# Turning the keys of a causal retention and gated-unit kernel by DMA instead of TensorE

## The chip, the cores and the metric

The kernel runs on one core of one Trainium2 chip. The metric is the device time of one execution in microseconds; the profile's span is a little shorter, since it begins with the first and ends with the last instruction on the engines. Engines are named as in the profile: PE is TensorE (PEld its weight loads), DVE is VectorE, ACT is ScalarE, POOL is GpSimd, SP is SyncE, which only issues DMAs. A small q behind an engine's name (SPq) means its queue of instructions that issue DMAs.

## The reference

The first part is retention: attention without softmax, in which the weight of a pair of positions decays with their distance. The second part is a gated linear unit whose gate is a causal convolution over five positions.

```python
# q, k, v: (8 batches, 8 heads, 576 positions, 64), float32
scores = q @ k.transpose(0, 1, 3, 2) / sqrt(64)
gamma  = 1 - 2 ** (-5 - arange(8))                 # one per head
Dmat   = where(i >= j, gamma ** (i - j), 0)        # i, j: positions
x      = ((scores * Dmat) @ v)                     # then heads side by side: (8, 576, 512)

gate_pre = sum(conv_w[kk] * x_padded[:, kk:kk + 576, :] for kk in range(5))
gate     = 1 / (1 + exp(-gate_pre))
val      = x @ w_val                               # w_val: 512 x 512
out      = (gate * val) @ w_out                    # w_out: 512 x 512, float32
```

## The kernel before

The positions are worked through in chunks of 128: four full ones in each batch, and the last 64 positions of two batches together as one "tail". That makes 36 chunks, numbered t = 0 to 35. Inside a chunk the scores are computed and masked; what earlier chunks contribute comes through a carried state (keys times values, summed). The decay is folded into the values (on GpSimd) and into the result.

For the scores TensorE needs queries and keys with the head dimension across the partitions, but they are loaded with the position there. So both are turned. Four transposes of 128x128 (two heads each) go through TensorE against an identity matrix into PSUM, and VectorE copies the result to SBUF (queries: ScalarE):

```python
        def turned(src, pool=None):                                   # L241 is the transpose below
            ps = pool.tile([P, NP, P], BF16, name="g") if pool else ps_t.tile([P, NP, P], BF16, name="tps")
            flat = src.rearrange("p h d -> p (h d)")
            for pr in range(NP):                                      # NP = 4
                nc.tensor.transpose(ps[:, pr, :], flat[:, pr * P:(pr + 1) * P], ident)
            return ps

        def turn_k(t, copy=nc.vector.tensor_copy):
            ps = turned(kbf[t])
            kt = tp_sb.tile([P, NP, P], BF16, name="kt")
            copy(kt, ps)                                              # L249
            ktd[t] = kt
```

Loads. Values (and the queries of tails) come through SyncE's queue in float32; the queries of the four full chunks of a batch come in one DMA of 1 MB. Keys come through GpSimd's queue, whose DMAs convert to bfloat16 on the way:

```python
        def load_one(name, src, kind, b, c, bufs):
            t = half.tile([P, H, D], F32, name=f"f{name}c", bufs=bufs)
            if kind == "full":
                nc.sync.dma_start(out=t, in_=src[b, :, c * P:(c + 1) * P, :].rearrange("h p d -> p h d"))
            # ... tails: two halves

        def load_keys(t):
            kb = bfp.tile([P, H, D], BF16, name="kb", bufs=LA + 3)    # LA = 8
            if kind == "full":
                nc.gpsimd.dma_start(out=kb, in_=k[b, :, c * P:(c + 1) * P, :].rearrange("h p d -> p h d"))
            # ... tails: two halves
            kbf[t] = kb
```

The first chunks are written out by hand, with much preparation between them. The steady part is this loop; each engine takes its own instructions out of it in this order. A unit n of the gated part covers two chunks; its convolution and value product run in an even iteration, its projection in the odd one after it.

```python
        for t in range(4, NT + 2):                                    # NT = 36
            n = t // 2 - 1
            # ...
            for b in qload.get(t, []):
                load_queries(b)                                       # SyncE, 1 MB
            if ok(t + LA - 2):
                load(t + LA - 2)                                      # SyncE: values of chunk t + 6
            if ok(t + 4):
                load_keys(t + 4)                                      # GpSimd
            if ok(t + 2):
                cast_v(t + 2)                                         # GpSimd: decay into the values
            for job in qjobs.get(t + 1, []):
                cast_q(job)                                           # GpSimd: queries to bfloat16
            if ok(t):
                take_state(t)
            if ok(t + 1):
                scores(t + 1)                                         # TensorE, needs ktd[t + 1]
                masks(t + 1, 0)
            if ok(t):
                values(t)
                if not odd:
                    take_x(t)
            # ... second mask
            if unit and not odd and n > 1:
                conv(n)                                               # TensorE, tiles of 64x64
                gate(n, 0)
                gate(n, 1)
            if ok(t + 2) and t > 4:
                turn_k(t + 2)                                         # TensorE and VectorE
            # ...
            part = project if odd else value
            if unit and t > 4:
                part(n, 0)
            # ...
            if jobs:
                turn_q(jobs[0])
            if unit and t > 4:
                part(n, 1)
            # ...
            if ok(t + 1):
                carried(t + 1)
                update(t + 1)
```

`project` ends with a copy on ScalarE and the store of 128 finished positions on SyncE's queue:

```python
            ob = op_sb.tile([P, DM], F32, name="ob")                  # 5 buffers
            nc.scalar.copy(ob, o)                                     # L414
            if kind == "full":
                c0 = (c + i) * P
                nc.sync.dma_start(out=out[b, c0:c0 + P, :], in_=ob)   # L417
```

Of the kernel before, what the change touches and what calls it, by code (L numbers as in the profile page):

```python
# [14 lines left out]
BF16 = mybir.dt.bfloat16  # L15
# [6 lines left out]
def kernel(  # L22
# [10 lines left out]
    nc = tc.nc  # L33
# [3 lines left out]
    P = 128  # L37
    NP = H // 2
# [13 lines left out]
    tp_sb = ctx.enter_context(tc.tile_pool(name="tsb", bufs=3))  # L52
# [16 lines left out]
    NT = len(chunks)  # L69

    with tc.manual_schedule():
# [13 lines left out]
        def load(t):  # L85
            kind, b, c = chunks[t]
            if kind == "tail":
                load_one("q", q, kind, b, c, 2)
            load_one("v", v, kind, b, c, LA + 1)

        def load_keys(t):

            kind, b, c = chunks[t]
            kb = bfp.tile([P, H, D], BF16, name="kb", bufs=LA + 3)
            if kind == "full":
                nc.gpsimd.dma_start(out=kb, in_=k[b, :, c * P:(c + 1) * P, :].rearrange("h p d -> p h d"))  # L96
            else:
                for i in range(2):
                    nc.gpsimd.dma_start(out=kb[i * TAIL:(i + 1) * TAIL],
                                        in_=k[b + i, :, c * P:S, :].rearrange("h p d -> p h d"))  # L100
            kbf[t] = kb

        kbf, vbf = {}, {}

        def load_queries(b):
            t = half.tile([P, H, RQ, D], F32, name="fqb", bufs=2)
            nc.sync.dma_start(out=t.rearrange("p h r d -> p h (r d)"),
                              in_=q[b, :, 0:RQ * P, :].rearrange("h (p r) d -> p h (r d)", r=RQ))
            loaded["qb", b] = t
# [109 lines left out]
        def cast_v(t, eng=nc.gpsimd):  # L219
            vb = bfp.tile([P, H, D], BF16, name="vb")  # L220
            eng.tensor_tensor(vb, loaded["v", *chunks[t]],  # L221
                                    gin[:, chunks[t][2], :].unsqueeze(2).to_broadcast([P, H, D]), op=ALU.mult)
            vbf[t] = vb
# [4 lines left out]
        def cast_q(job, copy=nc.gpsimd.tensor_copy):  # L228
            qb = bfp.tile([P, H, D], BF16, name="qb", bufs=5)
            if job[0] == "own":  # L230
                src = loaded["q", *chunks[job[1]]]
            else:
                src = loaded["qb", job[1]][:, :, job[2], :]
            copy(qb, src)  # L234
            qbf[job] = qb
# [6 lines left out]
            return ps  # L242

        ktd = {}

        def turn_k(t, copy=nc.vector.tensor_copy):
            ps = turned(kbf[t])
# [3 lines that stand above are left out]
# [22 lines left out]
        def scores(t, spare=False):  # L273
            kt = ktd[t]
            s = [ps_g.tile([P, NP, P], F32, name="g") if spare else ps_s.tile([P, NP, P], F32, name=f"s{i}")
                 for i in range(2)]
            for pr in range(NP):
                for i in range(2):
                    r = slice(i * 64, i * 64 + 64)
                    nc.tensor.matmul(s[i][:, pr, :], lhsT=kt[r, pr, :], rhs=queries(t, r, pr),  # L280
                                     start=(pr == 0), stop=(pr == NP - 1), skip_group_check=True)
            sps[t] = s
# [3 lines left out]
        def masks(t, i):  # L286
            m = mask_q if chunks[t][0] == "full" else mask_t
            p = pp.tile([P, NP, P], BF16, name=f"p{i}")
            nc.vector.tensor_tensor(p, sps[t][i], m.unsqueeze(1).to_broadcast([P, NP, P]), op=ALU.mult)  # L289
            pt[t, i] = p  # L290
# [22 lines left out]
        def values(t):  # L313
            kind, b, c = chunks[t]
            vb = vbf[t]
            o = ops[t]
            fresh = kind == "full" and c == 0
            for pr in range(NP):
                for i in range(2):
                    r = slice(i * 64, i * 64 + 64)  # L320
                    nc.tensor.matmul(o[r, pr, :], lhsT=vb[:, 2 * pr + i, :], rhs=pt[t, i][:, pr, :],  # L321
                                     start=(fresh and pr == 0), stop=(pr == NP - 1), skip_group_check=True)

        def take_x(t):
            kind, b, c = chunks[t]
            x = xg[b // GB]
            bl = b % GB
            if kind == "full":
                i0 = c * P
                by_token = lambda a: a.rearrange("p o (n r) -> p o n r", r=RQ)  # L330
                nc.vector.tensor_tensor(by_token(x[:, bl, :, PAD + i0:PAD + i0 + P]),  # L331
                                        ops[t].rearrange("p o (r n) -> p o n r", r=RQ),
                                        by_token(gout[:, :, i0:i0 + P]), op=ALU.mult)
            else:
                i0 = NCH * P
                for i in range(2):
                    nc.vector.tensor_tensor(x[:, bl + i, :, PAD + i0:PAD + S],
                                            ops[t][:, :, i * TAIL:(i + 1) * TAIL], gout[:, :, i0:S], op=ALU.mult)
# [17 lines left out]
        def take_state(t):  # L356
            kind, b, c = chunks[t]
            if kind != "full":
                return
            s = sbl[b % GB] if c == NCH - 1 else sbd[c % 2]  # L360
            for i in range(2):
                r = slice(i * 64, i * 64 + 64)
                nc.scalar.copy(s[r, :, i * 64:i * 64 + 64], st[b][r, :, i * 64:i * 64 + 64])  # L363
            state[b] = s
# [13 lines left out]
        def conv(n):  # L378
            g = [ps_g.tile([P, 2, 2 * P], F32, name="g") for _ in range(2)]
            lo, hi = slice(0, 64), slice(64, 128)  # L380
            for pr in range(2):
                a, b = 2 * pr, 2 * pr + 1
                for kk in range(KC):
                    for (rows, blk, cols, bank) in ((lo, a, lo, 0), (hi, b, lo, 1), (lo, b, hi, 0), (hi, a, hi, 1)):
                        nc.tensor.matmul(g[bank][cols, pr, :], lhsT=dg[rows, blk, kk, :], rhs=xs(n, rows, blk, kk),  # L385
                                         start=(pr == 0 and kk == 0), stop=(pr == 1 and kk == KC - 1),
                                         skip_group_check=True)
            gps[n] = g
            gsb[n] = []
# [33 lines left out]
        ok = lambda t: 0 <= t < NT  # L423
# [118 lines left out]
        for t in range(4, NT + 2):  # L542
            n = t // 2 - 1
            unit = n < NT // 2
            odd = t % 2 == 1
            jobs = qjobs.get(t, [])
            for b in qload.get(t, []):
                load_queries(b)
            if ok(t + LA - 2):
                load(t + LA - 2)  # L550
            if ok(t + 4):
                load_keys(t + 4)
            if ok(t + 2):
                cast_v(t + 2)
            for job in qjobs.get(t + 1, []):
                cast_q(job)
# [3 lines that stand above are left out]
                scores(t + 1)  # L560
# [5 lines that stand above are left out]
            if ok(t + 1) and not odd:  # L566
                masks(t + 1, 1)
            if unit and not odd and n > 1:
                conv(n)
                gate(n, 0)  # L570
                gate(n, 1)
            if ok(t + 2) and t > 4:
                turn_k(t + 2)
            if ok(t) and odd:
                take_x(t)
            if ok(t + 1) and odd:
                masks(t + 1, 1)
# [3 lines that stand above are left out]
            if t == 4:  # L581
                project(0, 0)
# [4 lines that stand above are left out]
            if t == 4:  # L587
                turn_k(6)
                project(0, 1)
            for job in jobs[1:]:  # L590
                turn_q(job)
# [3 lines that stand above are left out]
            if t == 5:  # L595
                nc.gpsimd.tensor_copy(mask_t, mask)
                nc.gpsimd.memset(mask_t[0:64, 64:128], 0.0)
# [28 lines left out]
```

## Time and profile before

Three runs gave 168.92, 169.11 and 169.61 us; the median is 169.11 us. The profiled execution has a span of 166.7 us.

| what | measured | how to read it |
|---|---|---|
| transposes of keys, TensorE (L241) | 144 instructions for 36 chunks | four for each chunk; matmuls follow each other in a pipeline, so their own durations (219 ns) overlap |
| copies of turned keys (L249) | 33 on VectorE, 423 ns each; 3 on ScalarE | PSUM to SBUF |
| SyncE's queue (q1) | 57,744 packets, 29.63 MB | values, queries, weights, results |
| GpSimd's queue (q0) | 36,000 packets, 4.98 MB | keys and one weight, in bfloat16 as written |
| HBM | 30.42 MB read, 9.44 MB written | 239 GB/s over the span |
| value load, 256 KB | 8.8 us from issue to landing (median of 32) | the DMA's time in the queue is in it |
| query load, 1 MB | 9.3 us (8) | |
| key load, 128 KB as written | 7.5 us (30) | |
| store, 256 KB | 5.7 us (32) | |
| waits of GpSimd | 13.1 us for query loads, 9.0 us for value loads | idle time of an engine that isn't the bound costs nothing by itself |

The page cuts the span into 40 equal slices and gives the busy share of each engine in tenths, one digit a slice, 9 standing for 90% or more. The row "DMA" is the mean over the core's 16 DMA engines. The chain that ended last is followed back from the last instruction: at each step to what released it, or to the instruction before it on the same engine.

### The profile page before, as it was taken

How to read it: one execution, taken by the hardware profiler on the slowest of the kernel's cores; microseconds unless marked ns; L12 is line 12 of the kernel's file. 1: busy time of each engine (PE TensorE's matmuls, PEld its weight loads, DVE VectorE, ACT ScalarE, POOL GpSimd, SP SyncE). 2: the span in 40 equal slices, each digit the busy share in tenths (PEclk: the TensorE clock that was granted, in tenths of full speed). 3: DMA queues.
4: the chain of work that ended last, by engine and by line, in shares of the span. 5: the costliest groups of instructions: out<-in, count | busy, mean ns of one | idle time of the engine just before them, and what ended most of it. 6: DMA issues, size and time to landing. Idle time of an engine off the chain costs nothing.

```text
span 166.7 us, 5543 instructions
## 1 busy us (share of the span) xinstructions
PE 153.5 (92%) x2297; PEld 110.2 (66%) x2297; DVE 114.2 (68%) x217; ACT 89.9 (54%) x183; POOL 99.4 (60%) x132
## 2 busy tenths in 40 slices
PE   6768878799999999999999999999999999999970
PEld 1344656556868777777868686868686877868630
DVE  6784673676677777768677777777777788686330
ACT  6934337446655557474546556565555563554430
POOL 7596999279699378675379286537977462000000
PEclk9999999999999999999999999999999999999999
DMA  5999999998999999999999999999999991303204
GB/s 112 301 264 253 294 213 288 226 162 238 275 263 287 247 236 214 174 258 267 267 163 246 268 274 188 216 285 289 233 259 187 212 236 42 130 0 130 97 33 126
DMA packets 93958, 35.23 MB, mean 211 GB/s; under 512 B 80090, under 2 KB 88814, under 8 KB 93934
## 3 DMA queue, kind: packets, MB, share of 16 engines
q1 hardware_dynamic: 57744, 29.63, 67.7%
q0 software_dynamic: 36000, 4.98, 44.0%
q8 instruction: 18, 0.29, 0.8%
q10 hardware_dynamic: 190, 0.27, 0.6%
q14 instruction: 6, 0.05, 0.1%
HBM read 30.42 MB, written 9.44 MB: 239 GB/s over the span
## 4 chain that ended last, share of the span: by engine, by line
PE 83%; ACT 4%; DVE 3%; POOL 3%; DMA 2%; issue 2%; ACTq 0%; DVEq 0%; POOLq 0%
PE g L400 18%; PE g L411 18%; PE g L385 13%; PE tps L241 10%; PE o L321 7%; PE s L280 7%; PE st L352 4%; PE o L304 3%; DMA fkc<-in_k_dram 2%; PE tps L445 1%; POOL dg L202 1%; ACT qtb L263 1%; DVE p L289 1%; DVE kt L249 1%; ACT ob L414 1%
## 5 line engine op out<-in xcount | busy, mean ns | idle before, releaser
L289 DVE TENSOR_TENSOR p<-s,maskq 128x512 bf16<-128x512 f32 x62 | 42.2, 685 | 17.6 <-PE s L280 17.5
L221 POOL TENSOR_TENSOR vb<-fvc,gin 128x512 bf16<-128x512 f32 x36 | 37.7, 1046 | 22.0 <-DMA fvc<-in_v_dram 9.0
L403 DVE TENSOR_TENSOR z<-gate,g 128x512 bf16<-128x512 f32 x36 | 24.7, 687 | 20.8 <-PE g L400 20.8
L400 PE MATMUL g<-xg,wvb 128*128 128x256 bf16 x288 | 36.9, 273 | 0.0
L411 PE MATMUL g<-wob,z 128*128 128x512 bf16 x144 | 36.5, 379 | 0.3 <-DVE z L403 0.3
L414 ACT COPY ob<-g 128x512 f32<-128x512 f32 x36 | 21.1, 585 | 28.3 <-PE g L411 28.0
L393 ACT ACTIVATE gate<-g 128x512 f32<-128x512 f32 x36 | 19.5, 594 | 19.1 <-PE g L385 19.1
L400 PEld LDWEIGHTS <-wvb 128*128 128x128 bf16 x288 | 26.6, 98 | 3.3 <-issue 0.6
L96 POOL DMA_DIRECT2D kb<-in_k_dram x30 | 28.4, 946 | 0.1
L234 POOL CAST qb<-fqb 128x512 bf16<-128x512 f32 x28 | 17.0, 620 | 13.1 <-DMA fqb<-in_q_dram 13.1
L385 PE MATMUL g<-xg,dg 64*64 64x256 bf16 x720 | 23.2, 271 | 0.0
L363 ACT CAST sbd<-st 64x256 bf16<-64x256 f32 x48 | 17.6, 366 | 8.8 <-PE st L352 8.3
L331 DVE TENSOR_TENSOR xg<-o,gout 128x512 bf16<-128x512 f32 x31 | 21.1, 681 | 1.3 <-PE o L321 1.3
L385 PEld LDWEIGHTS <-dg 64*64 64x64 bf16 x720 | 18.4, 106 | 2.3 <-issue 0.8
L411 PEld LDWEIGHTS <-z 128*128 128x128 bf16 x144 | 12.5, 98 | 10.4 <-DVE z L403 1.2
L263 ACT COPY qtb<-tps 128x512 bf16<-128x512 bf16 x24 | 14.1, 588 | 4.2 <-PE tps L241 4.2
L241 PE MATMUL tps<-ident,kb 128*128 128x128 bf16 x144 | 14.5, 224 | 0.8 <-DVE kb L216 0.8
L280 PE MATMUL s<-qtb,kt 64*128 64x128 bf16 x248 | 12.3, 219 | 2.5 <-DVE kt L249 1.1
L249 DVE COPY kt<-tps 128x512 bf16<-128x512 bf16 x33 | 14.0, 423 | 0.9 <-PE tps L241 0.7
L321 PE MATMUL o<-p,vb 128*64 128x128 bf16 x280 | 14.5, 225 | 0.0
L241 PEld LDWEIGHTS <-qb 128*128 128x128 bf16 x144 | 10.6, 98 | 5.4 <-issue 1.4
L352 PE MATMUL st<-vb,kb 128*128 128x128 bf16 x128 | 12.4, 219 | 0.7 <-POOL vb L221 0.7
(71 smaller groups left out, 142.0 us busy)
## 6 DMA issues: line engine op xcount, KB each, us to landing
fqb<-in_q_dram SPq DMA_DIRECT2D x8, 1024.0 KB, 9.3
fvc<-in_v_dram SPq DMA_DIRECT2D x32, 256.0 KB, 8.8
out_dram<-ob SPq DMA_DIRECT2D x32, 256.0 KB, 5.7
kb<-in_k_dram POOLq DMA_DIRECT2D x30, 128.0 KB, 7.5
wvf<-in_moe_w_val_dram SPq DMA_DIRECT2D x1, 1024.0 KB, 7.4
fqc<-in_q_dram SPq DMA_DIRECT2D x8, 128.0 KB, 5.2
fvc<-in_v_dram SPq DMA_DIRECT2D x8, 128.0 KB, 5.0
out_dram<-ob SPq DMA_DIRECT2D x6, 128.0 KB, 3.3
```

What stands on the lines that cost most here:

```text
L96: nc.gpsimd.dma_start(out=kb, in_=k[b, :, c * P:(c + 1) * P, :].rearrange("h p d -> p h d"))
L221: eng.tensor_tensor(vb, loaded["v", *chunks[t]], gin[:, chunks[t][2], :].unsqueeze(2).to_broadcast([P, H, D]), op=ALU.mult)
L241: nc.tensor.transpose(ps[:, pr, :], flat[:, pr * P:(pr + 1) * P], ident)
L280: nc.tensor.matmul(s[i][:, pr, :], lhsT=kt[r, pr, :], rhs=queries(t, r, pr), start=(pr == 0), stop=(pr == NP - 1), skip_group_check=True)
L289: nc.vector.tensor_tensor(p, sps[t][i], m.unsqueeze(1).to_broadcast([P, NP, P]), op=ALU.mult)
L321: nc.tensor.matmul(o[r, pr, :], lhsT=vb[:, 2 * pr + i, :], rhs=pt[t, i][:, pr, :], start=(fresh and pr == 0), stop=(pr == NP - 1), skip_gr ...
L331: nc.vector.tensor_tensor(by_token(x[:, bl, :, PAD + i0:PAD + i0 + P]), ops[t].rearrange("p o (r n) -> p o n r", r=RQ), by_token(gout[:, : ...
L385: nc.tensor.matmul(g[bank][cols, pr, :], lhsT=dg[rows, blk, kk, :], rhs=xs(n, rows, blk, kk), start=(pr == 0 and kk == 0), stop=(pr == 1 a ...
L400: nc.tensor.matmul(vps[:, j, :], lhsT=wvb[:, o, 2 * i + j, :], rhs=xs(n, slice(0, P), o, PAD), start=(j == 0 and o == 0), stop=(j == 1 and ...
L403: nc.vector.tensor_tensor(z, gsb[n][i], vps, op=ALU.mult)
L411: nc.tensor.matmul(o, lhsT=zsb[n, j // 2][:, j % 2, i * P:(i + 1) * P], rhs=wob[:, j, :], start=(j == 0), stop=(j == NP - 1))
L414: nc.scalar.copy(ob, o)
```

## The change

From chunk 10 on the keys are no longer turned on TensorE. A DMA on SyncE's queue reads the bfloat16 keys out of SBUF and writes them transposed into a new SBUF tile of four buffers, from which the scores read. It is issued in iteration t for chunk t + 3; the scores of that chunk stand in iteration t + 2. For its sake the key loads are issued five chunks ahead instead of four, so that the DMA's source is there. TensorE gives up four transposes and VectorE one copy for each of these 26 chunks. The first ten chunks stay as they are.

```diff
--- before.py
+++ after.py
@@ -242,6 +242,13 @@
             return ps
 
         ktd = {}
+
+        TURN = 10
+
+        def send_k(t):
+            kt = tp_sb.tile([P, NP, P], BF16, name="ktd", bufs=4)
+            nc.sync.dma_start(out=kt, in_=kbf[t].rearrange("p h d -> p (h d)"), transpose=True)
+            ktd[t] = kt
 
         def turn_k(t, copy=nc.vector.tensor_copy):
             ps = turned(kbf[t])
@@ -548,8 +555,12 @@
                 load_queries(b)
             if ok(t + LA - 2):
                 load(t + LA - 2)
-            if ok(t + 4):
-                load_keys(t + 4)
+            if t == 4:
+                load_keys(8)
+            if ok(t + 5):
+                load_keys(t + 5)
+            if TURN <= t + 3 < NT:
+                send_k(t + 3)
             if ok(t + 2):
                 cast_v(t + 2)
             for job in qjobs.get(t + 1, []):
@@ -569,7 +580,7 @@
                 conv(n)
                 gate(n, 0)
                 gate(n, 1)
-            if ok(t + 2) and t > 4:
+            if t > 4 and t + 2 < TURN:
                 turn_k(t + 2)
             if ok(t) and odd:
                 take_x(t)
```

## The prediction

> **What bounds the kernel now.** I read the engine table and the slices of the page first, then the chain that ended last, then the same chain piece by piece, and at the end the DMA side: windows, SyncE's queue and GpSimd in order of time.
>
> From the page, engines, slices and chain:
>
> ```profile
> PE 153.5 (92%) x2297; PEld 110.2 (66%) x2297; DVE 114.2 (68%) x217; ACT 89.9 (54%) x183; POOL 99.4 (60%) x132
> ...
> PE   6768878799999999999999999999999999999970
> ...
> DMA  5999999998999999999999999999999991303204
> ...
> PE 83%; ACT 4%; DVE 3%; POOL 3%; DMA 2%; issue 2%; ACTq 0%; DVEq 0%; POOLq 0%
> ```
>
> TensorE is busy nine tenths or more in every slice from the ninth to the thirty-eighth, and 83% of the chain is its own work: it is the bound. But the row of the DMA engines is as full, until slice 33 (about 134 us), when the last inputs are in. So two resources run side by side at their limit, and the change takes from the one and gives to the other.
>
> How full the DMA engines are shows in a window over the steady part. Its last three numbers are TensorE's clock, the DMA share (over 1 where packets of two queues lie over each other) and GB/s:
>
> ```profile
> 44.00:132.00 88.00, 87.77 (x1405) 66.58 (x1404) 66.06 (x113) 50.83 (x108) 61.58 (x75) 1.00 1.36 243
> ```
>
> I also cut 40 to 134 us into pieces of 1 us. Only 8 of the 94 have a share under 1.00, and the shortfalls add up to 1.4 us. That is all the idle time I can find on the DMA engines there, and 243 GB/s is what they deliver on this mix, in which keys and values come in packets of 256 bytes (64 floats of one head). The early stage, in which SyncE has nothing to wait for but room in its queue, runs no faster (264, 253 and 294 GB/s in slices 4 to 6, 213 in slice 7).
>
> The chain in pieces, in the middle and near the end (start, length, engine, tile, line):
>
> ```profile
> 104.08 1.22 PE g L385 x40
> 105.30 0.33 PE tps L241 x4
> 105.63 0.87 PE g L400 x8
> 106.51 0.22 PE tps L241 x4
> 106.73 0.87 PE g L400 x8
> ...
> 150.99 1.22 PE g L385 x40
> 152.21 1.85 PE g L400 x16
> ```
>
> The piece at 105.30 turns the keys of one chunk, that at 106.51 turns queries. The same four transposes take 0.33 us after the convolution, which works on 64x64 tiles, and 0.22 us after full-size matmuls. At 150.99 no keys are left to turn; there the two value steps take 1.85 us, where 2 x 0.87 = 1.74 is usual. So about 0.11 us belongs to the change from small tiles to the full array and stays when the transposes go: whoever comes next pays it.
>
> **What the Trainium skill says.** "VectorE: DVE Perf Modes", section "The three transpose paths", gives 390 ns for a 128x128 bf16 transpose on TensorE and 1309 ns by the DMA crossbar. The trace agrees with the first only for a transpose standing alone; in a stream four take 0.22 us, 55 ns each. The second no run here shows yet. "Advanced Engine Details and Errata", section "X-Bar Transpose (TRN2)", expects 350 to 400 GB/s of such DMAs, also not shown here. The two disagree by an order: 128 KB takes 0.33 to 0.37 us by the second, 4 x 1.309 = 5.2 us by the first if the four blocks go one after another. "DMA: Bandwidth & Descriptors", section "Issuing engines are not separate DMA queues", says that all queues end on the same 16 engines; the share of 1.36 with no faster flow agrees. Its section "Queues, rings and completion order" says that on each DMA engine a queue's descriptors are taken in the order of its ring, so a transpose on SyncE's queue stands behind the value and query loads issued before it.
>
> **The change, part by part.**
>
> Removed: the turning of chunks 10 to 35, 26 chunks. On TensorE 4 transposes each, worth 0.22 us net: 26 x 0.22 = 5.7 us, all on the path. On VectorE 26 copies of 423 ns (row of line 249): 11.0 us, off the path, since VectorE is busy 66.06 of 88 us in the window above and waits for TensorE. The ceiling of the gain is 5.7 us: 169.1 - 5.7 = 163.4 us. A pair of chunks takes 7.89 us now (convolutions start at 96.27, 104.08, 112.12 and 119.94) and would take 7.45.
>
> Added: 26 DMAs that read 128 x 512 bf16, 131 KB, and write as much. At the 243 GB/s of the window one takes 0.54 us of all 16 engines; at the skill's 350 to 400 GB/s an estimated 0.35. Some 23 of them come before the last inputs are in: 8.1 to 12.4 us of extra DMA time in a stage that has 1.4 us of it idle.
>
> Moved: key loads one chunk earlier on GpSimd's queue. This gives the crossbar its source in time: GpSimd issues key loads about 2 chunks ahead of TensorE as it is (the last at 129.8 us for a chunk whose turning runs at 147.9), and they land in 7.5 us. It moves no byte more.
>
> Sum. TensorE would want the inputs 23 x 0.22 = 5.1 us sooner by the end of loading; the DMA engines have them 8.1 - 1.4 = 6.7 to 12.4 - 1.4 = 11.0 us later. The gap is 11.8 to 16.1 us. Part of it is taken up by inputs that now come early. GpSimd, in order of time:
>
> ```profile
> 101.59 1.03 POOL L221 TENSOR_TENSOR vb<-fvc,gin 128x512 bf16<-128x512 f32 x1 [1.31 <-DMA fvc<-in_v_dram]
> ...
> 111.92 0.61 POOL L234 CAST qb<-fqb 128x512 bf16<-128x512 f32 x1 [2.48 <-DMA fqb<-in_q_dram]
> ```
>
> Both waits cost nothing now. By its place among the key loads the first is for chunk 24, whose value matmuls run at 111.78: 9 us of room. The second is for queries turned some 3 us later, as the first transposes of the iteration after the one at 112. I take the middle, 6 us. What is left, 5.8 to 10.1 us, stalls TensorE: 163.4 + 5.8 = 169.2 to 163.4 + 10.1 = 173.5 us. The middle is 171.3 us.
>
> **The rivals.**
>
> *The latency of one transpose sets the pace.* SyncE works in order, and its stores hold it back until ScalarE has the projected chunk:
>
> ```profile
> 103.31 0.59 SPq L78 DMA_DIRECT2D fvc<-in_v_dram  x1
> 103.99 0.63 SPq L107 DMA_DIRECT2D fqb<-in_q_dram  x1
> 104.67 1.58 SPq L78 DMA_DIRECT2D fvc<-in_v_dram  x1
> 106.34 3.05 SPq L417 DMA_DIRECT2D out_dram<-ob  x2
> ```
>
> The stores of an odd iteration are off at 103.3, as TensorE starts iteration 22 (scores at 103.41). Then come a value load and the new transpose, for chunk 25, whose scores stand at 111.45: two iterations, 7.45 us at the new pace. Against it stand 0.4 to 3 us to get the value load into the queue, and a landing that I put near that of its neighbours there (5.7 us for stores, 8.8 for values): L of 7 to 10 us. If L is over the pair's time, TensorE waits at the scores, and because every transpose waits for the stores of the pair before last, the pair settles at half of (7.45 + L), 3.7 + L/2. At L = 8.3 that equals today's 7.89; at 10 it is 8.7, some 13 x 0.8 = 11 us slower; behind one of the four 1 MB query loads (9.3 us to land) a single pair could lose 2 us or more. For it: queue order and the full DMA engines. Against: the second transpose of each pair has more room, and stores by then are often through. It would make 172 to 181 us, partly in place of the DMA deficit, not on top.
>
> *The crossbar is slow.* At the skill's 1309 ns per block in series, 5.2 us per chunk on a queue whose chunk lasts 3.9 us now, values and queries would starve: 26 x (5.2 - 1) is over 100 us in the worst case, half of it if other engines go on meanwhile. I give this kind of thing one in twelve.
>
> *The transposes are nearly free.* They never touch HBM, and if the limit of 243 GB/s lies in reading HBM in small packets, a copy from on-chip to on-chip memory may fit between. Then it is TensorE's saving alone, 163.4 us, or a little more for waits: 163 to 166. For it: windows of 1 us reach 363 and 380 GB/s when large packets are there, so the engines have more in them. Against: the share is over 1 nearly everywhere, so an engine with nothing to do is hard to find.
>
> **Range and chances.** The sum gives 169 to 173.5; the free transposes pull to 163.4, the latency and a slow crossbar pull far up. I say 171.3 us, and 164.0 to 184.0 for eight in ten. Faster by over 2% means under 165.7 us, so nearly the whole ceiling of 5.7 us must arrive: 0.22. Within 2%, 165.7 to 172.5: 0.33. Slower: 0.45.
>
> **What the profile after would show.** If I am right: the rows of line 249 fall from 33 copies on VectorE to 7, TensorE's transposes lose 104 instructions, TensorE's busy time falls by about 6 us while idle time before the scores (line 280) or before line 321 takes its place; the full part of the DMA row, which ends at about 134 us now, ends at 137 us or later; waits of GpSimd for the query and value loads, 13.1 and 9.0 us now, grow. If the latency rival is right, scores wait for the transposing DMA and the value loads do not wait more. If the transposes are free, the waits for DMA stay as they are and the pair takes 7.45 us. I would be wrong above all if the DMA engines have room that the share hides (time under 165), or if one transpose takes several us of a queue (time over 185).

## The result, and the profile after

The changed kernel takes 192.48 us (median; 191.96 to 194.96 over four runs) against 169.01 us for the kernel before: a ratio of 1.137, interval 1.133 to 1.141. It is 13.7% slower, and the prediction of 171.3 us with its range up to 184.0 us missed it.

The page of the changed kernel: engines, slices, the chain by engine and by line, two groups and the new DMA.

```profile
PE 150.3 (79%) x2173; PEld 105.7 (56%) x2193; DVE 103.5 (54%) x191; ACT 90.0 (47%) x183; POOL 99.3 (52%) x132
...
PE   5658887999900997887699599956999798999970
...
DMA  5999999999999999999999999999999999932114
...
DMA 42%; PE 36%; DVE 6%; SPq 5%; ACT 3%; issue 3%; POOL 2%; ACTq 0%; DVEq 0%; POOLq 0%
DMA ktd<-kb 32%; PE g L418 8%; PE g L392 8%; PE g L407 8%; DMA fqb<-in_q_dram 5%; DMA fvc<-in_v_dram 4%; PE s L287 4%; DVE p L296 3%; PE o L328 3%; SPq L78 2%; PE tps L241 2%; SPq L81 1%; PE st L359 1%; DVE z L410 1%; DVE xg L338 1%
```

TensorE no longer carries the chain: 36% of it instead of 83%, with 32% in the flight of the transposing DMAs. Its row has zeros in slices 12 and 13, where the first of them are due. The full part of the DMA row ends with slice 35, at about 166 us; before, it ended with slice 33, at about 137 us.

The waits of the changed kernel (total, times, longest), and a window over its loaded stage:

```profile
PEld L287 <- DMA ktd<-kb: 24.7, 12, 9.5
...
PE s L287 <- DMA ktd<-kb: 22.6, 10, 9.3
...
POOL qb L234 <- DMA fqb<-in_q_dram: 10.2, 5, 2.7
...
POOL vb L221 <- DMA fvc<-in_v_dram: 4.9, 3, 4.2
```

```profile
52.00:158.00 106.00, 82.85 (x1212) 59.38 (x1220) 54.08 (x86) 47.22 (x101) 55.77 (x68) 0.92 1.66 213
```

The first two lines are the same waits, seen by the weight load and by the matmul of the scores. GpSimd waits less for queries and values than before (13.1 and 9.0 us there), since TensorE is later. The window has the surprise: the DMA share rose from 1.36 to 1.66 and what the engines moved fell from 243 to 213 GB/s. TensorE's clock is 0.92 over it (1.00 before); it is low in and right after the slices in which TensorE stands idle. TensorE's whole busy time is 150.3 us, 2.5 us more than 153.5 less the 5.7 of the ceiling, so by this estimate the clock is worth 2.5 us at most.

SyncE's queue in order of time, and the chain beside it:

```profile
116.16 2.14 SPq L250 DMA_TRANSPOSE ktd<-kb  x1
118.40 0.55 SPq L107 DMA_DIRECT2D fqb<-in_q_dram  x1
119.00 0.69 SPq L78 DMA_DIRECT2D fvc<-in_v_dram  x1
119.79 4.39 SPq L250 DMA_TRANSPOSE ktd<-kb  x1
124.27 1.01 SPq L424 DMA_DIRECT2D out_dram<-ob  x2
```

```profile
114.84 1.22 PE g L392 x40
116.06 0.11 PE g L407
116.16 13.55 DMA ktd<-kb x2
129.76 0.44 PE s L287 x8
```

The transpose issued at 119.79, behind a 1 MB query load, holds SyncE's queue for 4.4 us, and the scores that need it run at 129.76. Between 52 and 134 us the pieces of that queue's timeline add up to 77 of 82 us, 45 of them in 17 transposes. A full queue alone explains nothing, though: in the kernel before the same sum is 75 us, and with plain copies in place of the transposes (e6, below) 80 us.

### The profile page after: what moved, and what is told of

Read it like the earlier page. It is cut to its first block, busy times and chain, and to the rows that moved or that the text cites. A ratio compares the mean times of both kernels' runs of the same rounds, so it can differ in the third digit from the quotient of the medians.

```text
span 190.3 us, 5350 instructions
## 1 busy us (share of the span) xinstructions
PE 150.3 (79%) x2173; PEld 105.7 (56%) x2193; DVE 103.5 (54%) x191; ACT 90.0 (47%) x183; POOL 99.3 (52%) x132
## 4 chain that ended last, share of the span: by engine, by line
DMA 42%; PE 36%; DVE 6%; SPq 5%; ACT 3%; issue 3%; POOL 2%; ACTq 0%; DVEq 0%; POOLq 0%
DMA ktd<-kb 32%; PE g L418 8%; PE g L392 8%; PE g L407 8%; DMA fqb<-in_q_dram 5%; DMA fvc<-in_v_dram 4%; PE s L287 4%; DVE p L296 3%; PE o L328 3%; SPq L78 2%; PE tps L241 2%; SPq L81 1%; PE st L359 1%; DVE z L410 1%; DVE xg L338 1%
## 5 line engine op out<-in xcount | busy, mean ns | idle before, releaser
L418 PE MATMUL g<-wob,z 128*128 128x512 bf16 x126 | 38.9, 413 | 1.8 <-DVE z L410 0.5
L410 DVE TENSOR_TENSOR z<-gate,g 128x512 bf16<-128x512 f32 x36 | 24.7, 687 | 23.5 <-PE g L407 23.5
L400 ACT ACTIVATE gate<-g 128x512 f32<-128x512 f32 x36 | 19.5, 594 | 24.4 <-PE g L392 24.4
L407 PEld LDWEIGHTS <-wvb 128*128 128x128 bf16 x288 | 26.1, 98 | 5.9 <-issue 3.2
L96 POOL DMA_DIRECT2D kb<-in_k_dram x30 | 28.3, 945 | 0.3 <-issue 0.2
L287 PE MATMUL s<-qtb,ktd 64*128 64x128 bf16 x176 | 9.0, 222 | 19.4 <-DMA ktd<-kb 19.3
L234 POOL CAST qb<-fqb 128x512 bf16<-128x512 f32 x28 | 17.0, 619 | 10.2 <-DMA fqb<-in_q_dram 10.2
L287 PEld LDWEIGHTS <-ktd 64*128 64x128 bf16 x208 | 6.0, 95 | 26.0 <-DMA ktd<-kb 24.7
L418 PEld LDWEIGHTS <-z 128*128 128x128 bf16 x144 | 12.8, 103 | 13.1 <-issue 2.3
L241 PEld LDWEIGHTS <-qb 128*128 128x128 bf16 x144 | 11.1, 102 | 7.4 <-issue 2.8
L241 PE MATMUL tps<-ident,qb 128*128 128x128 bf16 x124 | 12.7, 228 | 1.0 <-ACT kt L256 0.5
L359 PE MATMUL st<-vb,kb 128*128 128x128 bf16 x128 | 12.4, 219 | 1.1 <-POOL vb L221 1.1
```

The costliest lines, as they stand in the source:

```text
L407: nc.tensor.matmul(vps[:, j, :], lhsT=wvb[:, o, 2 * i + j, :], rhs=xs(n, slice(0, P), o, PAD), start=(j == 0 and o == 0), stop=(j == 1 and ...
L410: nc.vector.tensor_tensor(z, gsb[n][i], vps, op=ALU.mult)
L418: nc.tensor.matmul(o, lhsT=zsb[n, j // 2][:, j % 2, i * P:(i + 1) * P], rhs=wob[:, j, :], start=(j == 0), stop=(j == NP - 1))
```

## The experiments

Three theories, and a fourth that came from the second set of runs. **A**: the scores wait for the latency of a transpose that is issued too late. **B**: the DMA engines lack time for the bytes and packets. **C**: a transpose holds SyncE's queue, and loads and stores come late behind it. **D**: beside other traffic a transpose brings all DMA engines to a standstill for about a microsecond. Where a kernel leaves keys unturned or transposes unread, its edit says so.

### The transposes without their reader, and earlier

```diff
 # e1_unread: transposes issued as in the change, written to a tile that nobody reads
-            if t > 4 and t + 2 < TURN:
+            if ok(t + 2) and t > 4:
                 turn_k(t + 2)
```

> Every transposing DMA is issued as in the changed kernel, but nobody reads what it writes: TensorE still turns all keys, as before. Only the load on SyncE's queue and on the DMA engines is added to the kernel before. Theory A (the scores wait for the latency of one transpose that is issued too late; the engines could carry it): 168 to 173 us. Theory B (the DMA engines have no room for the extra traffic, so values and queries come late whoever reads the transposes): 185 us or more.

Measured: 182.24 us, ratio 1.069 (1.061 to 1.078). Just below what B called for, far over A: traffic and queue alone cost 12 us, although no scores wait.

```diff
 # e2_early2
-name="ktd", bufs=4        load_keys(t + 5)        send_k(t + 3)
+name="ktd", bufs=6        load_keys(t + 7)        send_k(t + 5)
```

> Each transposing DMA is issued two iterations sooner (chunk t + 5 instead of t + 3), its key load too, with six buffers instead of four. Same traffic, one more pair of chunks (7.5 us) to hide a landing of 6.0 us median and 9.6 us longest. Theory A: the waits of the scores for the DMA, 47 us over both TensorE queues, all but vanish and the time is 164 to 172 us. Theory B: 185 to 193 us, with waits for value and query loads in place of those.

Measured: 189.32 us, 1.111 (1.103 to 1.119), some 4 us better than the change and inside what B called for. The scores still wait 17.7 us, and GpSimd now 22.9 us for query and 19.1 us for value loads: what was sent sooner pushed back something else. A by itself falls.

The pace says the same. From the stores issued at 77.1 us to those at 159.9 us the changed kernel makes nine pairs of chunks, 9.2 us each; the unread form makes nine from 77.6 to 160.1 us, 9.2 each. With or without a reader the loaded stage has one pace (7.9 us before). The reader adds that TensorE follows at a greater distance: from that last point to the end of the span it takes 30 us with and 20 us without.

### The parts that should be free

```diff
 # e3_no_turn: leaves out the turning of chunks 10 to 35; their scores use chunk 9's keys
-            kt = ktd[t]
+            kt = ktd[min(t, TURN - 1)]
 # e4_keys5: no transposing DMA, all keys turned on TensorE, key loads five ahead
```

> Chunks 10 to 35 are not turned by anybody: their scores use the turned keys of chunk 9. No transposing DMA, no TensorE transposes and no copies of them for these chunks: the ceiling of the change. Both theories: 163.4 us by the net 0.22 us per chunk; 160.5 us if all of the 0.33 us in the chain went away.

> Only the second part of the change: key loads five chunks ahead, all keys turned on TensorE as before. Both theories: 169 us, within 0.5 us of before, as it moves no byte more and SyncE's queue is the same. A fall of this part would be a time over 171 us.

Measured: 165.33 us (0.974, 0.966 to 0.982) without any turning, 169.39 us (0.998, 0.995 to 1.002) with the earlier key loads alone. The ceiling is a saving of 4.4 us (3.0 to 5.7), so the net 0.22 us per chunk (5.7 us) was at the upper edge of it. The moved key loads cost nothing.

### The cost of one, by itself

```diff
 # e5_alone: the kernel before, and behind its end
+        for i in range(8):
+            nc.sync.dma_start(out=turn[i], in_=kbf[NT - 2].rearrange("p h d -> p (h d)"), transpose=True)
+        for i in range(8):
+            nc.sync.dma_start(out=lone[i][:, :, 0:P], in_=turn[i])      # pieces of 256 bytes
```

> The kernel before, and behind its last store eight transposing DMAs and then eight plain copies of the same 131 KB from SBUF to SBUF, in 512 pieces of 256 bytes each, all on SyncE's queue with nothing else on the DMA engines. It measures the disputed cost by itself. Theory B (a transpose takes much time of the DMA engines): transposes follow each other at 1.5 us or more, the copies at well under 1 us. Theory C (a transpose holds SyncE's queue, the engines have little work with it): SyncE is held 1.2 us and more by each, and between them the engines stand idle for most of the time. If the first guess (0.35 to 0.54 us of engine time) were right, neither would show over 0.6 us.

SyncE's queue, and two windows, the first with transposes alone, the second with copies alone:

```profile
164.17 10.69 SPq L601 DMA_TRANSPOSE turn<-kb  x8
174.91 5.53 SPq L603 DMA_DIRECT2D lone<-turn  x8
```

```profile
166.50:174.50 8.00, 0.00 (x0) 0.00 (x0) 0.00 (x0) 0.00 (x0) 0.00 (x0) 0.50 0.50 100
175.50:181.50 6.00, 0.00 (x0) 0.00 (x0) 0.00 (x0) 0.00 (x0) 0.00 (x0) 0.50 0.80 168
```

A transpose comes every 1.34 us, and holds SyncE for 1.27 us of that (the median of the eight); a copy comes every 0.69 us. The engines are busy half of the time in the first window, 0.50 x 1.34 = 0.67 us per transpose, and 0.80 x 0.69 = 0.55 us per copy. So alone a transpose costs the engines hardly more than its bytes. It lands in 2.4 us. B had asked for 1.5 us or more from one to the next, C for a hold of 1.2 us and idle engines: here C's sign came, so C had to be followed up. The 1309 ns per block that the Trainium skill gives ("VectorE: DVE Perf Modes", section "The three transpose paths") do not add up over the four blocks of one DMA. Nor did the prediction's 350 to 400 GB/s come: 100 GB/s in the first window, with the engines half idle.

### Copies in place of transposes

```diff
 # e6_copy256: as e1_unread, but
-nc.sync.dma_start(out=kt, in_=kbf[t].rearrange("p h d -> p (h d)"), transpose=True)
+nc.sync.dma_start(out=kt[:, :, 0:P], in_=kbf[t].rearrange("p (o i) d -> p o (i d)", o=NP))
```

> As the run with unread transposes (182.2 us), but each transpose is replaced by a plain copy of the same keys from SBUF to SBUF on the same queue, in 512 pieces of 256 bytes. Theory B by packets (any 512 packets cost this much): 180 to 184 us. Theory B or C by the crossbar's own way (what the transpose does, not its bytes or packets, costs): 169 to 173 us.

Measured: 172.27 us, 1.015 (1.008 to 1.023). This is the run that splits the loss: the same bytes, pieces, places and queue cost 2.6 us, and what makes them transposes costs another 9 us (1.069 against 1.015). Bytes and packets (B) are the small part. The profile of the copies is of the longest of their four runs, 173.84 us. Windows over the loaded stage of the two, copies first, transposes (e1_unread) second:

```profile
52.00:142.00 90.00, 86.27 (x1364) 64.58 (x1374) 65.13 (x112) 49.23 (x104) 54.36 (x66) 1.00 1.33 237
```

```profile
52.00:158.00 106.00, 97.94 (x1537) 73.42 (x1534) 73.11 (x126) 55.08 (x116) 55.72 (x68) 1.00 1.71 211
```

With copies the share stays at 1.33 and the flow at 237 GB/s. With transposes the engines look busier and move less.

### Other queues

```diff
 # e7_split: as e1_unread; SyncE keeps the transposes, loads and stores go to ScalarE's queue
 # e9_act_unread: as e1_unread, transposes to ScalarE's queue at the end of the iteration
+            if TURN <= t + 6 < NT:
+                send_k(t + 6)                    # nc.scalar.dma_start(..., transpose=True), keys seven ahead
 # e10_act_read: the same, and the scores read them
 # e11_stores_act: the changed kernel, stores on ScalarE's queue
```

> As the run with unread transposes (182.2 us), but in the loop SyncE's queue has the transposes alone: value loads, query loads and stores are issued from ScalarE's queue. Same traffic on the same DMA engines. Theory C (loads and stores stand behind a held SyncE): 168 to 174 us. Theory B (the engines are short of time): 180 us or more. ScalarE's own issue time, some 45 us more on an engine busy 90 of 180 us, may add a few us in either case.

> The unread transposes once more (182.2 us on SyncE's queue), but issued from ScalarE's queue, at the end of each iteration, for chunk t + 6 with key loads seven ahead, so that their keys are there. Loads and stores stay on SyncE. Same bytes on the same 16 DMA engines. Theory C (a transpose holds SyncE's queue for 2.4 us in the loaded stage, the queue fills, and loads and stores come late behind it): 169 to 175 us, near the 172.3 us of the plain copies. Theory B (the DMA engines lack the time): 180 us or more.

> The changed kernel with the transposes issued from ScalarE's queue at the end of each iteration, for chunk t + 6, key loads seven ahead, seven iterations' worth of room for the landing (six buffers); the scores read them. Theory C: TensorE's saving of some 4 to 6 us against the unread form of the same, 164 to 170 us. Theory B: 180 us or more, as its traffic is unchanged.

> The changed kernel (192.5 us), transposes on SyncE's queue as there, but the stores of finished positions issued from ScalarE's queue, right behind the copy that they wait for. It takes 1 us of issue per pair of chunks off SyncE, and its waits for ScalarE. Theory C: SyncE is full for about 11 pairs in the loaded stage, so 178 to 186 us. Theory B: 190 to 195 us, as no traffic is taken away.

Measured: 212.72 us (e7), 197.05 us (e9), 195.52 us (e10) and 204.01 us (e11, 200.07 to 205.65). All got worse, and none came near what C called for. But two queues bring something else in: the DMAs of SyncE and ScalarE take turns at eight completion semaphores, each waiting until the one eight before it has landed. In e7 ScalarE stood behind transposes that waited for their keys (97.7 us of waits of SyncE's queue for key loads). In e9 ScalarE stops ahead of transposes that it issues itself, three times before a cast and once before a gate (total, times, longest; in e10 four times, 28.3 us):

```profile
ACT sbd L369 <- issue: 17.3, 3, 7.0
...
ACT gate L399 <- issue: 6.5, 1, 6.5
```

So none of the four decides about C. Two things can still be read from them. In e10 the trace has no wait of the scores for a transpose left, and the time is 195.52 us: a late reader is not needed for a loss of this size. And in e9 SyncE has over 50 us of waits for ScalarE, as in the kernel before, so its queue is not what is short. Yet the loads of the loop take longer to land than in the kernel before (9.3 us for queries and 8.8 us for values there); landing is the last number:

```profile
fqb<-in_q_dram SPq DMA_DIRECT2D x8, 1024.0 KB, 12.4
fvc<-in_v_dram SPq DMA_DIRECT2D x32, 256.0 KB, 9.8
```

With SyncE's queue relieved, the transfers themselves are slower. That points at the engines, though not at bytes.

### The standstills

Windows of 0.25 us of the changed kernel show what the slices hide:

```profile
99.25:99.50 0.25, 0.25 (x9) 0.24 (x7) 0.00 (x0) 0.01 (x1) 0.00 (x0) 1.00 1.20 265
99.50:99.75 0.25, 0.25 (x13) 0.20 (x11) 0.13 (x1) 0.00 (x0) 0.00 (x0) 1.00 8.70 216
99.75:100.00 0.25, 0.25 (x8) 0.15 (x8) 0.25 (x1) 0.00 (x0) 0.00 (x0) 1.00 0.08 17
100.00:100.25 0.25, 0.25 (x12) 0.25 (x8) 0.25 (x2) 0.00 (x0) 0.00 (x0) 1.00 0.17 27
100.25:100.50 0.25, 0.25 (x8) 0.12 (x4) 0.25 (x2) 0.00 (x0) 0.00 (x0) 1.00 0.16 27
...
100.75:101.00 0.25, 0.21 (x1) 0.10 (x1) 0.25 (x2) 0.00 (x0) 0.25 (x1) 1.00 0.07 16
101.00:101.25 0.25, 0.25 (x3) 0.12 (x2) 0.25 (x2) 0.00 (x0) 0.25 (x1) 1.00 0.76 236
```

At 99.7 us some 20 packets begin that do not end until 101.2 (their whole length is booked in the window where they begin: hence 8.70), and for 1.25 us next to nothing moves: 16 to 30 GB/s, what one or two engines of the 16 do at the usual 213. Then the flow is back at once.

I counted such standstills in the packet records of the traces: nine or more packets on any queue that overlap and take over 0.4 us each, instruction loads not counted, from 45 us on. In the kernel before, a packet of 256 bytes takes 18 ns (median) and none over 71 ns.

| run | transposes | standstills, total us | time, us |
|---|---|---|---|
| before | 0 | 0 | 169.0 |
| no turning (e3) | 0 | 0 | 165.3 |
| keys earlier (e4) | 0 | 0 | 169.4 |
| copies (e6) | 0 | 0 | 172.3 |
| change | 26 | 13, 19.4 | 192.5 |
| unread (e1) | 26 | 16, 21.2 | 182.2 |
| two iterations sooner (e2) | 26 | 14, 19.5 | 189.3 |
| ScalarE's queue, unread (e9) | 26 | 15, 22.5 | 197.1 |
| from chunk 23 (e8) | 13 | 7, 9.7 | 178.9 |
| two chunks in one DMA, unread (e13) | 13 | 10, 17.1 | 179.2 |
| last three chunks (e14) | 3 | 0 | 168.3 |

Every kernel with transposes in the loaded stage has them (e7, e10 and e11 too: 12, 18 and 15), no other has one.

The flow of bytes shows how much hangs on them. Between 52 and 158 us the standstills make up 17.9 us of the change and 19.7 us of e1_unread. Outside them the engines move 246 GB/s in both, against 243 in the kernel before, by the same packet records. So the whole fall to 213 and 211 GB/s lies inside the standstills. If a queue held by its transposes (C) starved the engines, the flow outside the standstills would be thinner too, and it is not.

The two runs with half the transposes:

```diff
 # e8_turn23
-        TURN = 10
+        TURN = 23
 # e13_pair_unread: as e1_unread, keys of two chunks in one tile, one transpose for both
-            nc.sync.dma_start(out=kt, in_=kbf[t].rearrange("p h d -> p (h d)"), transpose=True)
+            nc.sync.dma_start(out=kt, in_=kbp[t - 1].rearrange("p j h d -> p (j h d)"), transpose=True)
```

> The changed kernel with the transposing DMAs from chunk 23 on, 13 of them instead of 26. Both theories: the loss of 23.5 us is in proportion to the number of transposes that fall into the loaded stage (10 of 23), 178 to 181 us. If only the early ones hurt (the stage in which loads catch up): 170 us or less.

> As the run with unread transposes (182.2 us), but one transposing DMA for two chunks, 262 KB each, 13 instead of 26; the keys of two chunks share a tile. Same bytes, same packets. Theory D: half the standstills, so about half of the 10 us by which the transposes cost more than the plain copies (172.3 us): 175 to 179 us. Theory B (bytes) or C (SyncE held in proportion to the bytes): 181 to 184 us.

Measured: 178.92 us (1.055, 1.047 to 1.063) with 13 of 26 transposes, a little under half of the loss with half of the standstills; and 179.19 us (1.057, 1.050 to 1.063) with all bytes in 13 DMAs. The second is at the edge of what D expected: fewer standstills, but longer ones (17.1 us for ten), so that only 2 to 3 of the 9 us came back.

### What brings them about

Three stretches of 16 steps behind the end of the kernel before, with the DMA engines to themselves: loads; loads and a transpose; loads and a copy.

```diff
 # e12_mixed: for each of three phases, 16 steps
+                load_keys(...)                                             # GpSimd, four steps ahead
+                load_one("v", v, "full", j % 8, j % 4, LA + 1)             # SyncE, 256 KB
+                # phase 1: transpose of the keys; phase 2: copy of them in 256-byte pieces
 # e15_mixstore
+                nc.sync.dma_start(out=away[phase * N + j], in_=held)       # a store of 256 KB each step
 # e16_mixquery
+                if j % 4 == 0:
+                    load_queries(j // 4)                                   # 1 MB every fourth step
 # e17_mixone
+                if j % 4 == 3:                                             # twice 8 KB into one partition
+                    nc.sync.dma_start(out=one[part], in_=v[0, part, 0:32, :].rearrange("s d -> (s d)").unsqueeze(0))
```

> The kernel before, and behind its last store three stretches of 16 steps on the DMA engines alone: (1) a value load of 256 KB on SyncE and a key load on GpSimd; (2) the same and a transposing DMA of keys loaded four steps earlier; (3) the same and the plain copy of 131 KB in 256-byte pieces in its place. It shows what a transpose costs beside loads. Theory D (beside other traffic a transpose brings all 16 engines to a standstill for 1 to 3 us, in about every second one; alone it costs 0.67 us): stretch 2 takes 1.2 us or more per step over stretch 1, with packets of over 0.4 us in it, and stretch 3 about 0.6 us more than stretch 1, without such packets. Theory B (bytes and packets alone): stretch 2 and 3 take the same.

> The three stretches of the mixed run (value and key loads; the same with a transpose; the same with a plain copy), each step with a store of 256 KB from SBUF to HBM as well, as the kernel has. In the mixed run 2 of 16 transposes went with a standstill of all engines, and a step with a transpose took no longer than one with a copy (2.5 us). Theory D with unequal queues (a transpose needs all 16 engines at once and they come to it at different times when the traffic is mixed): standstills of over 0.4 us in 5 or more of 16 steps, and the step 0.5 us longer than with a copy. If stores don't matter: 0 to 3 standstills.

> The same three stretches with a query load of 1 MB in every fourth step in place of the stores. Theory D with unequal queues: 4 or more standstills in the 16 steps with a transpose, none in those with a copy. If queries don't matter: 0 to 3.

> The same three stretches with two loads of 8 KB into one partition in every fourth step, ahead of the transpose, so that one DMA engine of the 16 comes about 1 us late to it. It stands for the loads of instructions, 16 KB in one packet of about 1 us, which the trace shows right before many of the standstills. Theory D: a standstill of 0.4 us and more at each of the four transposes that follow such a load, none with copies. If a late engine does not hold up the others: 0 to 2.

Measured, standstills in the three stretches by the same count: e12 0, 2, 0; e15 0, 2, 0 (of 0.5 us each); e16 1, 8, 0; e17 0, 3, 0. The one in e16's first stretch (198.5 to 201.5 us) is no stop: ten packets of 1 KB take long there while the engines go on moving about 245 GB/s. The eight among e16's transposes leave 86 to 126 GB/s, so they are shallower than those of the change, which leave 53 on average. The last of them begins at 267.0 us, 3.1 us after the last transpose was issued and before the first copy was.

My expectation for e12 was wrong: beside even traffic a transpose rarely stops anything. Its 16 steps with transposes issued in 40.9 us (from 193.16 to 234.05 us), 2.56 us a step; the copies took 2.58 us a step over their first eight, while key loads still came. Stores don't do it either. 1 MB loads in the queue do, eight times with transposes and never with copies, as D expected. Each of these four runs is a single execution.

e17 was to show whether one long packet is enough, and it is not. D expected a standstill of each pair of 8 KB packets. Five pairs run beside or just ahead of the transposes, at 196.4 (the last of the stretch before), 203.8, 217.4, 228.7 and 240.0 us; only the first two are followed by a standstill, at 197.5 (0.9 us) and 205.4 us (2.2 us). The third standstill, at 212.1 us (0.8 us), comes after another long packet, an 8 KB load of instructions at 211.5 us. So each standstill begins 0.6 to 1.6 us after a long packet has begun, and three of the five pairs make none. In the stretch with copies no pair (250.9, 262.9, 269.7, 276.7 us) makes one. A long packet is not needed either: none of the eight standstills in e16 has one of 8 KB or more within the 6 us before it. In e12 one of the two standstills (222.4 us) has its nearest long packet 2.3 us before it, the other (202.6 us) has none nearby. In the kernels a load of instructions, one packet of 16 KB and about 1 us, is often at hand: 5 of the 13 standstills of the change and 7 of 16 in e1_unread begin within 1.5 us of its start.

What brings a standstill about is therefore settled only in part: a transpose in flight is needed, large loads in the queue make it frequent, and a long packet can be ahead of it but is neither enough nor needed. One reading is that a transpose needs the engines together, and those that reach it first stand still, with all their queues, until the last is there. It fits the 16 to 30 GB/s of the laggards and the alone and even cases with little or no loss; e17 fits it only in part. It is argued, not shown, since the records used here don't name the engine, and it stays open.

### A version that is faster than both

```diff
 # e14_turn33
-        TURN = 10
+        TURN = 33
```

> The changed kernel with transposing DMAs for the last three chunks alone, which are issued when the last inputs have been loaded and the DMA engines are at 0.3 to 0.5 of their share. All theories: 168.2 to 169.2 us, 0.5 us saved on TensorE at best; over 170 us if even there a transpose lands too late for its scores.

Measured: 168.32 us, 0.993 (0.990 to 0.996) over five rounds, a gain of 0.7%. Only chunks 33 to 35 are turned by DMA, when the loads are over. The trace on the tile of turned keys: how long each of the three holds SyncE (ns, least, median and most), the first and last start (us), and in the second line the time from issue to landing.

```profile
L250 SPq DMA_TRANSPOSE ktd<-kb x3: 1222/1230/1297, 138.8 to 145.3; - x3
...
DMA to landing us min/median/max: 2.4/2.7/3.7
```

They hold SyncE no longer than the transposes of e5 did on idle engines, and no standstill is among their packets.

## Why the prediction was wrong

**What bounds the kernel.** Right: TensorE and the DMA engines side by side. The change took from the one and overloaded the other. Two readings were off, without weight in the sum: the full part of the DMA row ends with slice 33, at about 137 us and not 134, so an end at "137 us or later" was no sign of anything (it came at 166); and the 264, 253 and 294 GB/s are slices 3 to 5, the 213 slice 6.

**What is removed.** About right: 4.4 us (3.0 to 5.7) measured for the 5.7 us ceiling. The removed copies on VectorE mattered no more than said.

**What is added: the step that failed.** The prediction put one transposing DMA at 0.35 to 0.54 us of all engines, by its bytes. As bytes that was fair: 0.67 us alone, and 26 copies of the same bytes cost 2.6 us of the total, where its sum gives 12.4 - 1.4 - 6 = 5.0 us. But the transposes cost 9 us more than the copies (1.069 against 1.015). Missing was the standstill of the engines, 19 to 21 us over 26 transposes, 0.7 to 0.8 us each, more than the bytes themselves. That the flow is lost in the standstills is shown; that they make up all of the 9 us is argued, since no run takes them away and leaves the transposes in the loaded stage.

In the prediction's sum 0.54 + 0.75 = 1.29 us for each of 23 gives 29.7 us instead of 12.4, and 163.4 + (5.1 + 29.7 - 1.4 - 6) = 190.8 us, near the 192.5 measured. That closeness is luck: the same sum would put the unread form at about 191 us too, and it took 182.2. Why it stays below is not shown; the inputs that come early may take up more than the 6 us I allowed.

**What is moved.** Right: earlier key loads are free (e4).

**The rival of the latency: the second step that failed.** It was real, and was set aside wrongly as "partly in place of the DMA deficit, not on top". It is on top. Unread 1.069, read 1.137: 11.4 us more although TensorE does 4.4 us less, so about 16 us for waiting. But it does not set the pace, as that rival had it; the pace of 9.2 us a pair is the same unread. It sets how far TensorE trails behind, and sending earlier got back only 4 us, as other inputs then came later (e2). So the 23.5 us are some 2.6 for the bytes, 9 for what makes them transposes and 11.4 for the reader, net of TensorE's saving.

**The slow crossbar** at 5.2 us per chunk did not happen; **nearly free** transposes exist only where the loads are over (e14).

**What the profile would show.** VectorE's copies fell from 33 to 7 as said, and the scores wait. The sign named for the DMA deficit, longer waits of GpSimd for queries and values, did not come (10.2 and 4.9 us, less than before). By the prediction's own test that speaks for the latency of the transposes. The sign came in the unread form, where TensorE does not wait for them (17.0 and 16.5 us), so the reader hid it; the fall of the DMA flow from 243 to 213 GB/s was the plainer sign, and the prediction did not name it.

**The range.** Its upper end of 184 us left out that two of the rivals could add up. Engines at a share of 1.36 with 1.4 us to spare should have made any unknown of the new operation count against the change more widely than 0.45 for slower.

## What to carry to other kernels

Before moving work from a full engine to DMA, replace it by a plain copy of the same bytes and look at both: here the copy cost 1.5% and the transpose 7%, and only the pair told bytes from behaviour. A transposing DMA belongs where little else is in flight; it was free for the last three chunks and ruinous in the stage where queries of 1 MB, values and keys fill the queues. Where the DMA share rose and GB/s fell, as here, the engines were waiting and not working, and windows of a fraction of a microsecond showed it.

## What was not expected of the hardware

- Transposes in the traffic of this kernel stop nearly all DMA engines for 0.5 to 3.7 us at a time (7 to 16 times in the tabled runs with 13 or 26 of them), on every queue, while the same transposes alone keep the engines busy half of the time and stop nothing.
- A transposing DMA of 131 KB holds the queue of its issuer 1.2 us even with idle engines, a copy 0.65 us; behind loads in the same queue the transposes of e1_unread held it for 2.4 us (median), up to 4.0.
- The Trainium skill ("DMA: Bandwidth & Descriptors", section "Rules for kernel authors") says that a transpose next to ordinary DMAs needs nothing. The rule is about waits that keep data right and says nothing of time: next to this kernel's loads 26 transposes cost 9 us over copies.
